# One fitted table of small steps for units 14 to 23, the change of stages and the first pass of the last stage of a linear-attention and MoE kernel

## The chip, the cores and the metric

The kernel runs on one core of a Trainium2 chip. The metric is device time in microseconds (us) of one execution, the median of three runs. The five engines of the core are named as the profile names them: PE (TensorE, matrix products; PEld is its loading of weights), DVE (VectorE), ACT (ScalarE), POOL (GpSimd) and SP (SyncE, which here issues most of the transfers). PSUM is the memory that PE writes into, eight banks of 128 x 512 floats; SBUF is the working memory of all the engines.

## The reference

Three layers, each fed by the one before; 3072 tokens (4 sequences of 768) of 384 values:

```python
# linear attention with a decaying state, 8 heads of 48
cur = einsum('bhd,bhe->bhde', u[None] * kt, vt)
y[:, :, t] = einsum('bhd,bhde->bhe', rt, state + cur)
state = wt[:, :, :, None] * state + einsum('bhd,bhe->bhde', kt, vt)
...
# layer 1: 384 -> 1024 -> 384
h = x @ w_in
e = exp(h - max(h));  sm = e / (sum(e) + 1e-09)
solu = h * sm
ln = (solu - mean(solu)) / sqrt(var(solu) + 1e-06) * g_ln
x = ln @ w_out
...
# layer 2: 384 -> 2048 -> 384
h = x @ w_in
g = maximum(0.01 * h, h)
out = g @ w_out
```

The weights of both layers come as 64-bit floats.

## The kernel before

**Number format.** Every large product is made in three passes: each operand is split into a high part (a rounded copy) and a low part (the rest), and high x high, low x high and high x low are added up in PSUM. A layer's weights come as pairs of 32-bit words and are decoded on the chip, slice by slice of 128 x 384 values: `decode_exp` (one operation on DVE, L114, then one on ACT, L116), `decode_sign` (DVE L120), `decode_top` (DVE L125), `decode_sum` (DVE L131), `decode_mul` (DVE L136), then a copy to the high part on ACT (L772) and a subtraction on DVE for the low part (L773). Layer 2 has 32 such slices, 16 of `w_in` and 16 of `w_out`. A raw slice sits in one of 4 buffers `w2s`, its decoded value in one of 3 buffers `w2t`.

**Units.** The tokens go through attention and layer 1 in 24 units of 128. A unit's steps are small functions. Preparation of decays and keys (`prep1` to `prep4`, `prep_state` and others) is made two or three units ahead, on DVE, ACT and POOL. Then come the attention products on PE (`att_scores`, `att_mid`, `att_y`, `att_state`), the sum `x` (`att_x`), its transpose and split (`x_t`, `x_hi`, `x_lo`), and layer 1's first product (`mm1`, 18 matmuls, L566) into the PSUM tile PH. On this stand the softmax and its statistics: `soft_max` (DVE), `soft_e` (ACT), `soft_z` (DVE), `soft_nm` (POOL), `soft_c` (ACT), `soft_q` (ACT). The result is transposed into the two banks PZ (`z_t`, eight transposes, L596) and split (`z_hi` on ACT L605, `z_lo` on DVE L609). For each group g of three units, layer 1's second product (`mm2`, L619) is made for three row blocks m of 24 matmuls each, some units later; `mm2_out` stores it to memory.

**Last stage.** Layer 2 has 96 items n, each a pair (g, c) of a group of 512 tokens and a block of 128 of the 2048 inner values. Items 0 to 31 alternate between groups 0 and 1 while the weights are decoded (the first pass); items 32 to 95 go through groups 2 to 5 one by one. An item is `mm3` (9 matmuls into a bank h, L794), 0.01 h on ACT (L801), the maximum on DVE (L802), the high part `gh` on ACT (L803), the low part `gw` on DVE (`gw_sub`, L808), and `mm4` (9 matmuls into three accumulator banks, L818), which stands two items later in PE's order.

**What sets the order.** The kernel is recorded with a manual schedule: each engine executes its instructions in the order in which the code calls the steps, and waits where an operand is not ready. Units 0 to 9 are ordered by a fitted table, the string `FIRST`. Units 10 to 22 repeat one line of steps, `LOOP`. Unit 23 and the change of stages (the last two softmaxes, `mm2` of the blocks 19 to 23, the closing and opening of memory pools, the first slices of layer 2's weights) are written out by hand, and the last stage is a loop whose body holds, for each of the 96 items,

```python
dec_step()
mm3(g, c)
gw_sub(g, c)
...
if 2 <= n < len(order) - 1:
    mm4(*order[n - 2])
```

where `dec_step` issues the whole decoding of one slice (its L114 and the second half of the slice before) as one block. Two PSUM pools of the last stage (two banks h, two sets of three accumulators) are opened when the pool of the units is closed.

Of the kernel before, what the change touches and what calls it, by code (L numbers as in the profile page):

```python
# [19 lines left out]
TOK = B * S  # L20
# [10 lines left out]
FIRST_UNITS = 10  # L31
FIRST = """
# [51 lines left out]
z_lo -1 0; z_lo -1 1; soft_q -1; prep_bonus 3; prep_check 3; mm1 0 0; mm1 0 1; prep1 3; prep2 3; prep_k 3  # L84
"""
# [225 lines left out]
def body(tc, trw, nat_q, nat_v, w1p, u_p, g_p, r, k, v, w, u, w1i, w1o, gln, w2i, w2o, out):  # L311
# [6 lines left out]
    with ExitStack() as ctx:  # L318
# [221 lines left out]
        def att_x(i):  # L540
            x = ap2.tile([128, H, D], F32, name="x")
# [171 lines left out]
        es2 = ExitStack()  # L713
        x2, acc, gs = {}, {}, {}
        lp_at = []
        wl = [("i", c) for c in range(3)]
        for c in range(K2):
            wl += [("o", c)] + [("i", c + 3)] * (c + 3 < K2)
        wd, wa, ws = [], [], []
        w2o_at, xhl2 = [], []  # L720

        def load_w2():
            if not wl:
                return
# [36 lines left out]
        def split_hi():
            if not ws or (ws[0][0] == "o" and ws[0][1] >= 4 * len(w2o_at)):
                return None
            s, c, t = ws.pop(0)
# [18 lines left out]
        def x2_lo(g, eng):  # L783
            xh, xl = x2[g]
            eng.tensor_tensor(out=xl, in0=f(xl), in1=f(xh), op=ALU.subtract)  # L785

        def mm3(g, c):
            xh, xl = x2[g]
            h2 = ps_h.tile([128, 512], F32, name="h2")
            v, o = divmod(c, 4)  # L790
            q = 0
            for kc in range(KC):
                for a, d in passes(w2i_h[v], w2i_l[v], xh, xl):
                    pe.matmul(out=h2, lhsT=a[:, kc, 128 * o:128 * o + 128], rhs=d[:, kc],  # L794
                              start=(q == 0), stop=(q == 8))
# [36 lines left out]

        with tc.manual_schedule():
# [25 lines left out]
            def mm2_of(i):  # L859
# [198 lines left out]
```

## Time and profile before

| | |
|---|---|
| median of three runs | 783.81 us (782.85 to 786.02) |
| the profiled execution | 783.52 us |
| its span, first to last instruction | 781.8 us |
| mean granted clock of PE | 0.988 |
| PE busy with matmuls | 730.4 us, 93% of the span |
| DVE busy | 518.5 us, 66% |
| ACT, POOL busy | 354.2 us and 162.6 us |

The profile is of one execution. The span is what the engines' records cover; 1.7 us of the execution's time lie around it. "Busy" is the time in which at least one instruction of the engine runs; matmuls overlap one another, so that a stretch in which PE shows no idle time can still take longer than its matmuls need. The granted clock is the share of TensorE's full clock that the chip allowed. In the middle of the kernel five points of the program are used as borders: 218.10 us, where the attention output of unit 14 begins, 326.70 us, where `mm1` of unit 22 begins, 366.04 us, where the last stage's first `mm3` begins, 494.20 us, where `mm3` of item 28 begins, and 776.00 us, the end of PE's work.

### The profile page before, as it was taken

Reading aid. Unit: us, or ns where it says so; the run is one execution under the profiler, and the core shown is the slowest. Engines: PE = TensorE matmul, PEld = TensorE weight load, DVE = VectorE, ACT = ScalarE, POOL = GpSimd, SP = SyncE. Lnnn points to the kernel's source line nnn. Section 1 sums busy time; section 2 is a strip of 40 time slices with the busy share of each in tenths; the row PEclk is TensorE's granted clock in tenths of the full one; section 3 lists DMA queues with packets and bytes.
Section 4 is the critical chain, followed back from the end, with each engine's and each line's share of the span. In section 5 each row is a group of like instructions: output and inputs, shape, how many; then the busy total and the mean of one; then the engine's idle time right before and its main releaser. Section 6 shows DMA issues by size and latency. Waiting matters only on the chain.

```text
span 781.8 us, 14968 instructions
## 1 busy us (share of the span) xinstructions
PE 730.4 (93%) x6197; PEld 612.9 (78%) x6197; DVE 518.5 (66%) x866; ACT 354.2 (45%) x648; POOL 162.6 (21%) x181
## 2 busy tenths in 40 slices
PE   2688999999999999989979999999999999999996
PEld 1366789898989999879758866788888888888885
DVE  6999889787888888577888888553343334334333
ACT  2557564666556465464444444433323322333231
POOL 2331554445555464002000000100100100100000
PEclk9999999999999999998989999999999999999999
DMA  9652335345354541035334221130002001001001
GB/s 299 201 164 71 99 102 161 92 139 146 98 161 127 164 117 48 22 92 162 91 113 162 81 81 41 37 125 1 0 3 79 0 1 42 0 1 41 0 1 44
DMA packets 30189, 66.60 MB, mean 85 GB/s; under 512 B 3228, under 2 KB 15668, under 8 KB 29988
## 3 DMA queue, kind: packets, MB, share of 16 engines
q1 hardware_dynamic: 29300, 62.45, 26.2%
q10 hardware_dynamic: 816, 3.15, 1.2%
q8 instruction: 50, 0.82, 0.5%
q14 instruction: 23, 0.19, 0.1%
HBM read 56.13 MB, written 9.45 MB: 84 GB/s over the span
## 4 chain that ended last, share of the span: by engine, by line
PE 72%; DVE 18%; issue 4%; ACT 3%; DMA 2%; POOL 0%; DVEq 0%; ACTq 0%; POOLq 0%
PE acc L818 18%; PE h L794 18%; PE PH L566 12%; PE PO L619 11%; PE PZ L596 3%; PE PZ L528 2%; DVE t L802 2%; ACT gh L803 2%; DVE w2s L131 2%; DVE w2t L120 2%; DMA ub<-in_u_p_dram 2%; PE PZ L537 1%; PE PA L465 1%; DVE gw L808 1%; DVE w2s L125 1%
## 5 line engine op out<-in xcount | busy, mean ns | idle before, releaser
L802 DVE TENSOR_TENSOR t<-t,h 128x512 f32<-128x512 f32 x96 | 65.8, 685 | 122.8 <-ACT t L801 122.8
L794 PE MATMUL h<-x2h,w2ih 128*128 128x512 f32 x288 | 114.8, 399 | 7.2 <-DVE t L802 7.0
L801 ACT ACTIVATE t<-h 128x512 f32<-128x512 f32 x96 | 57.1, 595 | 136.8 <-PE h L794 136.8
L808 DVE TENSOR_TENSOR gw<-t,gh 128x512 fp32r<-128x512 f32 x96 | 69.3, 722 | 65.9 <-ACT gh L803 65.9
L794 PE MATMUL h<-x2l,w2ih 128*128 128x512 f32 x288 | 112.7, 391 | 0.0
L794 PE MATMUL h<-x2h,w2il 128*128 128x512 f32 x288 | 112.7, 391 | 0.0
L818 PE MATMUL acc<-gw,w2oh 128*128 128x512 f32 x288 | 112.5, 391 | 0.0
L818 PE MATMUL acc<-gh,w2ol 128*128 128x512 f32 x288 | 112.5, 391 | 0.0
L818 PE MATMUL acc<-gh,w2oh 128*128 128x512 f32 x288 | 112.5, 390 | 0.0
L803 ACT CAST gh<-t 128x512 fp32r<-128x512 f32 x96 | 59.6, 621 | 93.8 <-DVE t L802 93.8
L785 POOL TENSOR_TENSOR x2l<-x2l,x2h 128x1536 fp32r<-128x1536 f32 x4 | 14.0, 3510 | 298.1 <-ACT x2h L781 298.1
L794 PEld LDWEIGHTS h<-x2h,w2ih 128*128 128x128 f32 x288 | 54.4, 189 | 25.8 <-DVE t L802 15.1
L794 PEld LDWEIGHTS h<-x2h,w2il 128*128 128x128 f32 x288 | 54.4, 189 | 11.5
L818 PEld LDWEIGHTS acc<-gh,w2ol 128*128 128x128 f32 x288 | 54.4, 189 | 11.3
L818 PEld LDWEIGHTS acc<-gw,w2oh 128*128 128x128 f32 x288 | 54.2, 188 | 11.3
L794 PEld LDWEIGHTS h<-x2l,w2ih 128*128 128x128 f32 x288 | 54.5, 189 | 10.8
L818 PEld LDWEIGHTS acc<-gh,w2oh 128*128 128x128 f32 x288 | 54.2, 188 | 11.2
L566 PE MATMUL PH<-w1ih,xh 128*128 128x512 f32 x144 | 59.2, 411 | 3.9 <-DVE zbuf L578 3.4
L619 PE MATMUL PO<-zh,w1oh 128*128 128x384 f32 x168 | 59.9, 357 | 0.0
L566 PE MATMUL PH<-w1ih,xl 128*128 128x512 f32 x144 | 57.2, 397 | 0.8 <-DVE xl L558 0.8
L566 PE MATMUL PH<-w1il,xh 128*128 128x512 f32 x144 | 57.1, 397 | 0.0
L619 PE MATMUL PO<-zh,w1ol 128*128 128x384 f32 x168 | 56.4, 336 | 0.0
(154 smaller groups left out, 1432.2 us busy)
## 6 DMA issues: line engine op xcount, KB each, us to landing
tr<-in_trw_dram SPq DMA_DIRECT2D x23, 675.9 KB, 5.5
natq<-in_nat_q_dram SPq DMA_DIRECT2D x24, 384.0 KB, 5.5
w2s<-in_moe_w_in_dram SPq DMA_DIRECT2D x48, 128.0 KB, 2.3
w2s<-in_moe_w_out_dram SPq DMA_DIRECT2D x16, 384.0 KB, 3.1
natv<-in_nat_v_dram SPq DMA_DIRECT2D x24, 192.0 KB, 3.8
o_dram<-o SPq DMA_DIRECT2D x24, 192.0 KB, 1.9
x2l<-o_dram SPq DMA_DIRECT2D x6, 768.0 KB, 5.3
out_dram<-ot SPq DMA_DIRECT2D x18, 256.0 KB, 2.1
```

The costliest lines, as they stand in the source:

```text
L120: nc.vector.scalar_tensor_tensor(out=t, in0=q[:, :, 1], scalar=-2147483648, in1=t, op0=ALU.bitwise_and, op1=ALU.bitwise_or)
L131: nc.vector.scalar_tensor_tensor(out=f(lw), in0=lw.bitcast(U32), scalar=2.0 ** -32, in1=q[:, :, 1], op0=ALU.mult, op1=ALU.add)
L528: pe.matmul(out=y[64 * c:64 * c + 64, hs], lhsT=s[64 * c:64 * c + 64, x, q], rhs=a[64 * c:64 * c + 64, h], start=(h == 0), stop=False, ski ...
L566: pe.matmul(out=PH[:, half], lhsT=a[:, kc], rhs=c[:, kc, 512 * half:512 * half + 512], start=(n == 0), stop=(n == 8))
L596: pe.transpose(PZ[c // 4][:, 128 * (c % 4):128 * (c % 4) + 128], zbuf[:, 128 * c:128 * c + 128], ident)
L619: pe.matmul(out=o2[m], lhsT=a[:, c, 128 * m:128 * m + 128], rhs=d[:, c], start=(c == 0 and q == 0), stop=(c == K1 - 1 and q == 2))
L794: pe.matmul(out=h2, lhsT=a[:, kc, 128 * o:128 * o + 128], rhs=d[:, kc], start=(q == 0), stop=(q == 8))
L801: act.activation(out=t, in_=h2, func=AF.Copy, scale=0.01)
L802: dve.tensor_tensor(out=t, in0=t, in1=h2, op=ALU.max)
L803: act.copy(out=gh, in_=t)
L808: dve.tensor_tensor(out=gw, in0=t, in1=f(gh), op=ALU.subtract)
L818: pe.matmul(out=at, lhsT=a[:, c % 4, 128 * o:128 * o + 128], rhs=d, start=(c == 0 and q == 0), stop=(c == K2 - 1 and q == 2))
```

## The change

A second table, `LAST`, takes the place of `LOOP` for units 14 to 22, of the hand-written code for unit 23 and the change of stages, and of the loop for items 0 to 33 of the last stage. Its steps are smaller: a slice's decoding is eight steps (`w2_load`, `w2_a` the exponent, `w2_e` the sign, `w2_f` the top, `w2_h` the sum, `w2_b` the product, `w2_c` the high part, `w2_d` the low part), an item's work between its two products is four (`g_min`, `g_max`, `g_hi`, `g_lo`), and `mm3`, `mm4`, the opening of pools, the loads of `x2` and the two small computations `flag` and `scale` are steps of their own, in any order that the table names. From item 34 on the loop is as it was.

Beside the order: PSUM is one pool, the last stage uses banks of the units' tiles (h: PK and one of PZ; accumulators: PH, the other PZ, PO and PA); `mm2` of the blocks 19, 21 and 23 uses PA in place of PK; `w2t` has 4 buffers (3), `x` one (2), `t` 2 and `gh`, `gw` 3 each throughout; one pair of the weight tiles stands in another pool; the last two `mm4` take their accumulators in the order 1, 2, 0.

```diff
+LAST_UNITS = 14
+N_LAST = 34
+N_RP = 4
...
+LAST = """
+soft_max 13; att_u 15; soft_e 13; w2_load 0; prep3 16; att_scores 15; att_y 14; load_nat 17; att_x 14; mm2a 14; x_t
...
+soft_e 23; z_lo 22 0; mm2b 24; z_hi 22 1; w2_f 6; soft_z 23; z_lo 22 1; soft_nm 23; soft_c 23; z_t 23; w2_e 7; w2_h
+5; mm2_out 24; z_hi 23 0; z_lo 23 0; w2_f 7; x2_hi 0; z_hi 23 1; flag_b; mm2a 25; flag_c; soft_q 23; w2_h 6; w2_b 5;
+z_lo 23 1; mm2b 25; w2_b 6; w2_load 8; open_xp; x2_lo 0; w2_h 7; mm3 0; mm2a 26; w2_b 7; w2_c 4; g_min 0; scale_a;
+w2_d 4; g_max 0; load_x2 1; x2_hi 1; mm2b 26; g_hi 0; w2_c 5; w2_c 6; w2_a 8; x2_lo 1; w2_load 9; w2_d 5; mm3 1; mm3
...
+g_max 11; w2_b 18; g_hi 10; w2_load 21; w2_c 17; mm4 9; g_lo 10; w2_d 17; w2_f 19; g_min 12; g_max 12; g_hi 11; w2_h
+19; w2_a 21; g_lo 11; mm3 13; w2_c 18; w2_load 22; w2_e 20; g_hi 12; w2_b 19; w2_f 20; w2_h 20; mm3 14; w2_e 21;
...
 def mm2(g, m, part):
     zh, zl = zg[g]
     if part == 0:
-        o2[m] = (PK if 3 * g + m in (19, 21, 23) else PO)[:, 0:384]
+        o2[m] = (PA[:, 0] if 3 * g + m in (19, 21, 23) else PO)[:, 0:384]
...
+        h_at = [PK, PZ[1]]
+        acc_at = [[PH[:, 0], PH[:, 1], PZ[0]], [PO, PA[:, 0], PA[:, 1]]]
...
+        def g_min(n):
+            p = pools["rp" if n < N_RP else "lp"]
+            gs[n] = [p.tile([128, 512], d, name=x, bufs=2 if x == "t" else 3)
+                     for x, d in (("t", F32), ("gh", F32R), ("gw", F32R))]
+            act.activation(out=gs[n][0], in_=h_at[n % 2], func=AF.Copy, scale=0.01)
+
+        def g_max(n):
+            t = gs[n][0]
+            dve.tensor_tensor(out=t, in0=t, in1=h_at[n % 2], op=ALU.max)
+
+        def g_hi(n):
+            t, gh, _ = gs[n]
             act.copy(out=gh, in_=t)
-            gs[g, c] = (gh, gw, t)
...
+        def g_lo(n):
+            t, gh, gw = gs[n]
             dve.tensor_tensor(out=gw, in0=t, in1=f(gh), op=ALU.subtract)
...
             run(FIRST)
-            for i in range(FIRST_UNITS, NU - 1):
-                if 15 <= i < 19:
-                    load_w2()
+            for i in range(FIRST_UNITS, LAST_UNITS):
                 run(LOOP, i)
...
-            for n in range(len(order)):
...
-                dec_step()
-                mm3(g, c)
-                gw_sub(g, c)
...
+            run(LAST)
+            for n in range(N_LAST, len(order)):
                 g, c = order[n]
-                if 2 <= n < len(order) - 1:
-                    mm4(*order[n - 2])
+                mm3(n)
+                g_min(n)
+                g_max(n)
+                g_hi(n)
+                g_lo(n)
```

Three places show what this does to DVE's order. The first is the first pass of the last stage. Before, DVE's order there repeats this block once for every item (L114 to L136 and L773 decode a slice, L802 is the maximum and L808 the low part `gw`):

```order
L114 TENSOR_SCALAR w2t<-w2s 128x384
L120 SCALAR_TENSOR_TENSOR w2t<-w2s,w2t 128x384
L125 TENSOR_SCALAR w2s<-w2s 128x384
L131 SCALAR_TENSOR_TENSOR w2s<-w2s 128x384
L136 SCALAR_TENSOR_TENSOR w2t<-w2s,w2t 128x384
L773 TENSOR_TENSOR w2il_4332<-w2t,w2ih_4331 128x3x128
L802 TENSOR_TENSOR t<-t,h_4998 128x512
L808 TENSOR_TENSOR gw<-t,gh 128x512
```

In the changed kernel the same operations (L195, L201, L206, L212 and L217 decode, L844 is a slice's low part, L907 the maximum, L915 the low part `gw`) stand in the same region like this, around the maxima of two successive items:

```order
L195 TENSOR_SCALAR w2t<-w2s 128x384
L907 TENSOR_TENSOR t<-t,PZ_100 128x512
L844 TENSOR_TENSOR w2il_4540<-w2t,w2ih_4539 128x3x128
L212 SCALAR_TENSOR_TENSOR w2s<-w2s 128x384
L915 TENSOR_TENSOR gw<-t,gh 128x512
L217 SCALAR_TENSOR_TENSOR w2t<-w2s,w2t 128x384 x2
L201 SCALAR_TENSOR_TENSOR w2t<-w2s,w2t 128x384
L907 TENSOR_TENSOR t<-t,PK 128x512
L206 TENSOR_SCALAR w2s<-w2s 128x384
L195 TENSOR_SCALAR w2t<-w2s 128x384
L212 SCALAR_TENSOR_TENSOR w2s<-w2s 128x384
L844 TENSOR_TENSOR w2ol_4756<-w2t,w2oh_4755 128x384
```

Between an item's maximum and its low part there now stand operations of other slices and other items, where nothing stood before, and the operations of several slices in work are mixed instead of one slice being decoded in one block.

The second is in the units, from the softmax maximum of unit 19 on (L571; L543 and L544 make `x` of unit 20, L578 is `soft_z`, L558 `x_lo`, L474 and L497 belong to the attention, L397 to L445 to the preparation of later units). Before:

```order
L571 TENSOR_REDUCE nmax<-PH 128x1
L543 TENSOR_TENSOR x<-PZ_99,vd 128x384
L544 TENSOR_TENSOR x<-PZ_100,x 128x384
L474 COPY_PREDICATED ss_122<-mask,PA 128x512
L578 SCALAR_TENSOR_TENSOR zbuf,z_all<-PH,ebuf 128x1024
L497 TENSOR_TENSOR ao<-PA,ae 112x192
L415 SCALAR_TENSOR_TENSOR e_3885<-tr,e_112 112x520
L558 TENSOR_TENSOR xl<-PZ_99,xh 128x384
L424 TENSOR_TENSOR lt<-tr,e_3885 112x512
L445 TENSOR_REDUCE dg<-natq 128x8
```

In the changed kernel, from the same softmax maximum on (L652, with L624 and L625 for `x`, L659 for `soft_z`, L639 for `x_lo`, L555 and L578 for the attention, L478 to L496 for the preparation), and with L201 and L206 of two slices' decoding:

```order
L652 TENSOR_REDUCE nmax<-PH 128x1
L201 SCALAR_TENSOR_TENSOR w2t<-w2s,w2t 128x384
L206 TENSOR_SCALAR w2s<-w2s 128x384
L624 TENSOR_TENSOR x<-PZ_99,vd 128x384
L625 TENSOR_TENSOR x<-PZ_100,x 128x384
L659 SCALAR_TENSOR_TENSOR zbuf,z_all<-PH,ebuf 128x1024
L484 RECIPROCAL e_112<-suf 112x8
L578 TENSOR_TENSOR ao<-PA,ae 112x192
L555 COPY_PREDICATED ss_122<-mask,PA 128x512
L496 SCALAR_TENSOR_TENSOR e_3923<-tr,e_112 112x520
L639 TENSOR_TENSOR xl<-PZ_99,xh 128x384
L478 SCALAR_TENSOR_TENSOR suf<-tr,sel 112x520
```

Steps of layer 2's decoding, which before stood in the change of stages and behind it, now stand among those of the units. The third place is PE's order at the change of stages, of which the lines of the table in the diff above tell all: before, `mm3` of item 0 stood behind the last `mm2`; now it stands ahead of `mm2` of the blocks 22 and 23 (`mm2a 26` to `mm2b 27`).

## Rows read from the trace of the kernel before

**Rows 1.** Head of the page and its part 1, busy time by engine.

```profile
span 781.8 us, 14968 instructions
...
PE 730.4 (93%) x6197; PEld 612.9 (78%) x6197; DVE 518.5 (66%) x866; ACT 354.2 (45%) x648; POOL 162.6 (21%) x181
```

**Rows 2.** Windows view: length, busy of PE, PEld, DVE, ACT, POOL, clock, DMA share, GB/s.

```profile
105.06:167.85 62.79, 61.30 (x924) 54.85 (x923) 52.39 (x81) 36.98 (x73) 28.29 (x37) 1.00 0.42 122
218.10:326.70 108.60, 108.60 (x1663) 99.56 (x1663) 86.24 (x131) 60.00 (x114) 51.78 (x56) 1.00 0.37 106
326.70:366.04 39.34, 36.18 (x245) 33.42 (x243) 27.64 (x53) 20.27 (x35) 0.47 (x2) 0.91 0.34 106
366.04:494.20 128.16, 118.45 (x489) 91.58 (x489) 106.83 (x217) 57.64 (x109) 4.20 (x1) 0.97 0.30 94
494.20:776.00 281.80, 281.56 (x1242) 232.85 (x1241) 109.61 (x158) 90.11 (x144) 14.04 (x4) 1.00 0.07 24
350.90:356.50 5.60, 5.60 (x20) 5.60 (x19) 5.02 (x10) 2.56 (x4) 0.00 (x0) 0.50 0.77 237
```

**Rows 3.** Timeline of PE in the change of stages: start, busy, operation, idle before.

```profile
337.33 1.09 PE L596 MATMUL PZ<-ident,zbuf 128*128 128x128 f32 x8 [0.24 <-ACT zbuf L586]
...
342.39 0.33 PE L619 MATMUL PO<-zh,w1oh 128*128 128x384 f32 x1
...
346.40 0.34 PE L619 MATMUL PO<-zh,w1ol 128*128 128x384 f32 x1
347.93 1.09 PE L596 MATMUL PZ<-ident,zbuf 128*128 128x128 f32 x8 [1.20 <-ACT zbuf L586]
350.75 0.19 PE L937 MATMUL PA<-ones,anyf 128*1 128x1 f32 x2 [1.73 <-DVE anyf L936]
```

**Rows 4.** Chain of the last stage's steady part: start, length, piece.

```profile
496.28 2.04 PE acc L818 x9
```

**Rows 5.** Timeline of DVE in the last stage's first pass.

```profile
384.80 0.69 DVE L808 TENSOR_TENSOR gw<-t,gh 128x512 fp32r<-128x512 f32 x1 [0.69 <-ACT gh L803]
385.41 0.35 DVE L114 TENSOR_SCALAR w2t<-w2s 128x384 int32<-128x384 int32 x1
...
387.73 0.55 DVE L773 TENSOR_TENSOR w2il<-w2t,w2ih 128x384 fp32r<-128x384 f32 x1
388.20 0.68 DVE L802 TENSOR_TENSOR t<-t,h 128x512 f32<-128x512 f32 x1
389.56 0.69 DVE L808 TENSOR_TENSOR gw<-t,gh 128x512 fp32r<-128x512 f32 x1 [0.69 <-ACT gh L803]
```

**Rows 6.** Waits view, first pass of the last stage: total, times, longest.

```profile
DVE gw L808 <- ACT gh L803: 17.9, 26, 0.7
...
PE h L794 <- DVE t L802: 7.0, 16, 1.3
```

**Rows 7.** Timeline of PE: where attention's output of two successive units begins.

```profile
306.01 0.27 PE L518 MATMUL PZ<-zero 48*64 48x192 bf16 x2
318.57 0.27 PE L518 MATMUL PZ<-zero 48*64 48x192 bf16 x2
```

**Rows 8.** Windows view of the table at the kernel's start, columns as above.

```profile
20.00:80.00 60.00, 45.42 (x612) 32.43 (x611) 58.37 (x107) 36.85 (x76) 17.08 (x21) 0.97 0.48 148
```

**Rows 9.** Groups by line, window 20 to 80 us: count, busy, mean ns.

```profile
L424 DVE TENSOR_TENSOR lt<-tr,e 112x512 f32<-112x512 f32 x4 | 2.7, 682 | 0.0
```

**Rows 10.** The same group, window 218.1 to 326.7 us.

```profile
L424 DVE TENSOR_TENSOR lt<-tr,e 112x512 f32<-112x512 f32 x8 | 7.7, 968 | 0.0
```

**Rows 11.** DMA issues of the page: count, KB each, us to landing.

```profile
w2s<-in_moe_w_out_dram SPq DMA_DIRECT2D x16, 384.0 KB, 3.1
...
x2l<-o_dram SPq DMA_DIRECT2D x6, 768.0 KB, 5.3
```

**Rows 12.** Groups by line, window 218.1 to 326.7 us.

```profile
L609 DVE TENSOR_TENSOR zl<-PZ,zh 128x512 fp32r<-128x512 f32 x16 | 10.3, 686 | 2.7 <-ACT zh L605 2.7
...
L605 ACT CAST zh<-PZ 128x512 fp32r<-128x512 f32 x17 | 9.2, 589 | 0.0
```

More of the change, by code (lines that the diff above doesn't have):

```diff
@@ new lines @@
+soft_max 20; soft_q 19; att_state 20; prep_vd 21; att_scores 22; att_u 22; prep_diag 22; att_y 21; att_x 21; soft_e
+20; soft_z 20; mm2_out 20; w2_b 2; w2_load 5; att_kt 23; w2_c 0; prep2 23; mm2a 21; x_t 21; mm2b 21; x_hi 21; w2_d
+0; x_lo 21; soft_nm 20; att_mid 22; att_evac_s 22; soft_c 20; w2_c 1; mm2_out 21; mm1 21 0; prep_vd 22; prep3 23;
+soft_q 20; z_t 20; prep_state 23; mm1 21 1; w2_f 3; att_mul_next 22; z_hi 20 0; z_lo 20 0; z_hi 20 1; att_evac_k 23;
+att_u 23; w2_a 4; z_lo 20 1; prep4 23; att_y 22; att_scores 23; prep_bonus 23; w2_e 4; prep_check 22; soft_max 21;
@@ new lines @@
+w2_d 1; att_x 22; soft_e 21; mm2a 22; x_t 22; w2_load 6; soft_z 21; w2_a 5; soft_nm 21; att_evac_s 23; x_hi 22; x_lo
+22; w2_f 4; w2_h 3; mm2b 22; mm1 22 0; mm2_out 22; prep_diag 23; w2_b 3; prep_vd 23; w2_load 7; w2_e 5; soft_c 21;
+att_mid 23; att_mul_next 23; z_t 21; z_hi 21 0; z_hi 21 1; z_lo 21 0; mm1 22 1; prep_check 23; z_lo 21 1; att_y 23;
+soft_q 21; flag_a; soft_max 22; att_x 23; mm2a 23; att_state 21; x_t 23; w2_c 2; w2_h 4; w2_b 4; soft_e 22; open_rp;
+x_hi 23; soft_z 22; w2_c 3; x_lo 23; mm2b 23; w2_d 2; load_x2 0; mm2_out 23; w2_a 6; w2_d 3; soft_nm 22; mm1 23 0;
@@ new lines @@
+2; w2_d 6; w2_load 10; w2_c 7; mm2_out 25; g_min 1; w2_e 8; w2_load 11; w2_f 8; w2_h 8; g_lo 0; w2_a 9; g_max 1;
+w2_e 9; w2_f 9; g_min 2; g_max 2; g_hi 1; w2_a 10; w2_b 8; mm3 3; mm2_out 26; g_lo 1; g_hi 2; w2_c 8; mm3 4; mm2a
+27; w2_d 7; mm4 0; w2_h 9; w2_a 11; w2_e 10; w2_d 8; g_lo 2; w2_f 10; w2_b 9; w2_h 10; w2_e 11; w2_b 10; g_min 3;
+w2_c 9; w2_c 10; mm2b 27; w2_load 12; w2_load 13; g_max 3; w2_a 12; mm2_out 27; w2_f 11; w2_d 9; w2_e 12; open_lp;
+w2_h 11; g_min 4; w2_a 13; g_max 4; w2_load 14; w2_b 11; w2_f 12; w2_c 11; g_hi 3; mm3 5; w2_e 13; w2_h 12; g_lo 3;
@@ new lines @@
+w2_load 28; w2_h 25; w2_d 23; g_lo 17; mm3 19; mm3 20; w2_f 26; mm4 16; g_min 19; w2_a 27; g_lo 18; w2_h 26; w2_b
+25; g_max 19; mm4 17; w2_c 24; mm3 21; g_hi 19; g_min 20; g_max 20; w2_load 29; mm3 22; g_lo 19; mm4 18; w2_c 25;
+w2_d 24; g_min 21; g_hi 20; mm4 19; w2_b 26; w2_e 27; w2_d 25; w2_a 28; w2_c 26; w2_load 30; g_lo 20; g_max 21;
+g_min 22; w2_a 29; g_max 22; mm3 23; g_hi 21; mm3 24; w2_e 28; g_lo 21; w2_f 27; w2_h 27; w2_d 26; mm4 20; w2_f 28;
+w2_b 27; g_min 23; g_max 23; mm4 21; g_hi 22; w2_e 29; g_lo 22; g_min 24; w2_c 27; w2_h 28; mm3 25; g_max 24; w2_d
@@ L85 @@
+g_hi 30; g_lo 30; g_min 31; g_min 32; g_max 31; g_max 32; g_hi 31; mm3 33; g_lo 31; w2_d 31; mm4 30; g_min 33; g_hi
+32; g_max 33; g_hi 33; g_lo 32; load_x2 3; g_lo 33; mm4 31
 """
@@ L761, in split_hi, with w2_a, w2_e, w2_f @@
[L761 to L764, printed above, removed]
+                sp.dma_start(out=raw[n], in_=words(w2o[128 * c:128 * c + 128]))
+        def w2_a(n):
+            val[n] = we.tile([128, DM], I32, name="w2t", bufs=4)
+            decode_exp(nc, raw[n], val[n], ebias)
+        def w2_e(n):
+            decode_sign(nc, raw[n], val[n])
+        def w2_f(n):
+            decode_top(nc, raw[n])
```

311 lines of the change are left out of this document (141 added, 170 removed).

## The prediction

> **What bounds the kernel now.** I read the head of the page first: over the whole span of 781.8 us PE shows matmuls for 730.4 us, DVE is busy for 518.5 us [rows 1]. PE is the bound on average, but the average hides stages, so the next view is the windows cut at the borders that the change moves [rows 2]. From 218.10 to 326.70 us PE is busy for all of the 108.60 us, DVE for 86.24: a unit there costs what PE needs, 12.56 us from one attention output to the next [rows 7]. From 494.20 us on PE is busy for 281.56 of 281.80 us, and the chain there is PE alone, nine matmuls in 2.04 us after nine matmuls [rows 4]. Between these two stretches lie 39.34 us of the change of stages and 128.16 us of the last stage's first pass, and only there is anything to be had.
>
> In the change of stages the timeline of PE shows the places [rows 3]. PE waits 0.24 us ahead of the transposes of unit 22. After a block of 24 matmuls, first at 342.39, last at 346.40 us (24 in 4.18 us, 0.174 us each), the next work could begin at 346.57 and begins at 347.93 us: 1.36 us lost on the softmax of unit 23. The eight transposes that follow take as long as those of unit 22 did until `mm1` took over (337.33 to 338.18, so 0.85 us); the small flag product then begins at 350.75 in place of 348.80 us: 1.95 us. Right behind this idle time the granted clock falls to the lower of its two levels, half speed (1.2 in place of 2.4 GHz): in the 5.60 us from 350.90 on there are 20 matmuls, which at 0.174 us would take 3.5 us [rows 2, 3]. That is 2.1 us; the mean clock of the whole stretch, 0.91 of 39.34 us, allows 3.5; I take 2.7. Sum of the losses: 0.24 + 1.36 + 1.95 + 2.7 = 6.3 us.
>
> In the first pass, 28 `mm3` and 26 `mm4` begin between 366.04 and 494.20 us: 54 items of 2.04 us [rows 4] are 110.2 us, and the stretch takes 128.16 [rows 2]: 18.0 us lost, 4.77 us for a pair in place of 4.08. DVE sets this pace: the timeline shows its low parts `gw` at 384.80 and 389.56 us, 4.76 apart, with no gap except 0.69 us ahead of each, in which it waits for ACT's high part `gh` of the same item [rows 5]; the waits view has 26 such waits, 17.9 us in all, nearly the whole of the 18.0 [rows 6]. PE in turn waits for DVE's maximum, which frees the bank h: 7.0 us in 16 waits [rows 6]. So a serial hand-off, maximum to `gh` to `gw`, is paid once per item by the engine that sets the pace.
>
> Matmul records overlap, and PE's busy time in this window is 118.45 us [rows 2]; read by that, only 128.16 - 118.45 = 9.7 us could be won. The Trainium skill (Perfetto Trace Analysis, section Identifying the Most-Contended Engine) says that matmul busy time is no good measure of how near PE is to its limit, and that the busy time of weight loads is. By this rule PE's work here is 91.58 us at the steady stretch's share of 232.85 in 281.80, or 110.8 us, and 17.3 us are to be had; the trace agrees, since the count above gives 18.0.
>
> **The change part by part.** *What it removes.* If DVE never waits and PE is always fed, the stretch from 326.70 to `mm3` of item 28 falls by 6.3 + 18.0 = 24.3 us. Against the profiled execution's own 783.5 us (span 781.8 and 1.7 around it), this is a floor of 759.2. The median of the runs is 0.3 us above the profiled execution, which is nothing.
>
> *What it adds.* No arithmetic: the same 32 slices, the same items. It is DVE's load that decides whether PE can be fed. From 218.10 to 494.20 us DVE is busy for 86.24 + 27.64 + 106.83 = 220.7 us [rows 2]; the floor of this stretch is 276.1 - 24.3 = 251.8, so DVE would be 88% busy. By parts: ahead of the first `mm3` the table decodes 8 slices, two more than before, some 2.4 us of DVE each from 385.41 to 388.20 us [rows 5] less the part of a slice that overlaps, so 86.24 + 27.64 + 4.8 = 118.7 us. PE's time there is 147.94 - 6.3 less the 8.35 us of two blocks of `mm2` that now stand behind the first `mm3`, 133.3 us: 89%. The rest is 102 of 118.5 us, 86%. A table has been seen to run DVE fuller than this: 58.37 of 60.00 us near the kernel's start [rows 8], there with DVE and not PE as the bound.
>
> *What it moves.* `mm4` of an item stands not two but up to five items behind its `mm3`, so 12 to 20 us of PE work lie between the two, in which 0.01 h, maximum, `gh` and `gw` fit (0.6 + 0.69 + 0.6 + 0.69 us [rows 5, 12], with the waits for their turn). Between maximum and `gw` stand 1 to 6 us of other DVE work, so the 0.69 us of [rows 6] lie under it: cost nothing. If this cover is gone somewhere, it is 0.69 us per place. The decoding's hand-offs to ACT (the exponent, the high part) are covered in the same way by operations of other slices. A raw slice's buffer comes free at `w2_b` of the slice four ahead; from there to `w2_a` lie 2.8 us of DVE work at the least and mostly 5 to 11, against 3.1 us for a transfer [rows 11]: at most 0.3 us once, not carried. SP's queue holds only such loads, the stores of `mm2_out` and the two loads of `x2`, and none of them waits for something late. `x` with one buffer must wait for the transpose of the unit before, long over; nothing. PA in place of PK for three blocks of `mm2`: the attention's last use of PA, `att_mid 23`, stands well ahead of `mm2a 23` in the table; nothing. The order of the last two `mm4`: at most the length of one output, 0.1 us.
>
> *What stays or comes.* (1) `z_t 23` is followed on PE by `mm2a 25`, which reads z of unit 23. Its first half goes through ACT (0.589) and DVE (0.686 us [rows 12]) while half of the transposes, 0.43 us, go on: 0.8 us of wait. (2) The softmax of unit 23 stands behind less PE work than in the units; between nothing and the 1.36 us of before: 0.4. (3) `x2` of group 1 is loaded behind `open_xp`: 5.3 us [rows 11], then a high and a low part of three times 512 values each, at most 3 x 0.589 and 3 x 0.686 us [rows 12], 9.1 in all, against 8.3 us of PE work (`mm2b 25`, `mm3 0`, `mm2` of block 22) up to `mm3 1`: 0.8, between 0 and 2. (4) Items 1 to 4 have four `mm3` in a row on two banks h; a bank comes back after 0.6 + 0.69 us, inside the 2.04 us of the other bank's `mm3`, if ACT and DVE are at hand; between 0 and 2 us, I take 0.8. (5) The rest of 300 steps in a fixed order: the units without a table lose nothing visible on PE, so 0 to 4; I take 1.5. Sum 4.3 us. Predicted: 783.5 - 24.3 + 4.3 = **763.5 us**.
>
> **The rivals.** *DVE slows down beside GpSimd.* The decoding's operations now stand in the units, where POOL is busy for 51.78 of 108.60 us; in the first pass it was for 4.20 of 128.16 [rows 2]. One DVE operation with two SBUF operands shows what this can mean: 682 ns in one window, 968 in another with more POOL work [rows 9, 10]. Ahead of the first `mm3` the table has 27 decoding operations with two SBUF operands (8 `w2_e`, 8 `w2_h`, 7 `w2_b`, 4 `w2_d`); at 0.29 us more each they take 7.7 us more, and DVE's 118.7 of 133.3 us become 126.4, 95%, near the fullest seen. With no slack left, half or all of it shows: 3 to 8 us over the forecast, 766.5 to 771.5. The Trainium skill (SBUF — State Buffer, section SBUF: two separate sides) says that DVE with two SBUF inputs and a GpSimd operation reading SBUF lock each other out for a whole instruction. By that rule these 27 operations are exposed; the difference between the two rows agrees with it.
>
> *Only the change of stages gains.* If the table's first pass keeps DVE's 4.77 us for a pair, because its hand-offs are late again, 783.5 - 6.3 = 777 to 778 us. For it: two banks h as before. Against it: other work stands between maximum and `gw`.
>
> *No change.* What the first pass and the change of stages give is lost in units 14 to 22, which had nothing to lose but DVE's slack: 780 to 787.7. A drop of the clock there, as the one at 350.90 us, costs 2.1 to 3.5 us each time; some six would be needed.
>
> *Slower.* The order of each engine is now rigid at 132 hand-offs from DVE to ACT and back (32 from `w2_a` to `w2_e`, 32 from `w2_c` to `w2_d`, 34 from `g_min` to `g_max`, 34 from `g_hi` to `g_lo`). If the real durations differ so that each shows the 0.69 us of [rows 6], that is 91 us of DVE standing still. DVE has 251.8 - 220.7 = 31 us to spare, or up to 63, since records overlap by 0.08 us (384.80 + 0.69 against 385.41 [rows 5]) in some 400 instructions; with 47, 44 us are lost against 24.3 won: 803 us. It decides from a mean wait of (47 + 24.3) / 132 = 0.54 us on. Against it: one such wait per item is all that the worst stretch of before shows.
>
> **How the numbers follow.** The forecast, 760 to 766.5 us, has 0.58; DVE beside GpSimd 0.23; only the change of stages 0.05; no change 0.06; slower 0.08. A measurement of this kernel can tell about 0.5%, 3.9 us, from no change, so faster is below 779.9 us: 0.58 + 0.23 + 0.05 = 0.86; same 0.06; slower 0.08. The range from 759.5 (the floor) to 773 us holds the first two cases with their bounds, 0.81.
>
> **What would show it.** Right: PE's busy share near 1.00 in every window from unit 14 to item 34; item 28's `mm3` some 20 us earlier; no `gw` wait of 0.69 us per item; DVE near 88% from unit 14 on; no second half-speed stretch of the clock. The sizes of (1) to (4) are the idle times ahead of `mm2a 25`, `mm3 1` and `mm3 3`. Wrong: DVE's decoding operations longer by 0.2 us or more in the units and PE waiting there for `soft_max`, `x_lo` or `z_lo`; or a period near 4.77 us for a pair in the first pass.

## The result and the profile after

The changed kernel takes 766.13 us (median of four runs, 764.97 to 767.82), the kernel before 784.74 us on the same chip (four runs, 782.85 to 786.02): ratio 0.9766, 95% interval 0.9736 to 0.9796, so 2.3% faster. Forecast were 763.5 us and a range of 759.5 to 773. The profiled execution has a span of 764.9 us in place of 781.8 [rows 1].

The windows of the changed kernel, with the columns of [rows 2] and its borders where they now lie (the output of unit 14, `mm1` of unit 22, the first `mm3`, `mm3` of item 28, the end of PE):

```profile
219.69:328.11 108.42, 107.53 (x1605) 97.63 (x1597) 93.62 (x154) 60.60 (x115) 42.53 (x53) 1.00 0.38 115
328.11:357.07 28.96, 26.91 (x204) 23.56 (x204) 20.85 (x39) 18.93 (x33) 1.97 (x4) 1.00 0.37 118
357.07:472.03 114.96, 114.96 (x518) 96.10 (x518) 98.09 (x203) 59.45 (x109) 7.97 (x2) 1.00 0.31 102
472.03:757.80 285.77, 285.76 (x1261) 236.30 (x1259) 111.47 (x164) 88.99 (x143) 10.54 (x3) 1.00 0.07 23
```

The reader is to see three things. The first pass (third line) is 13.2 us shorter than before, and PE has no idle time in it; since two blocks of `mm2` (8.35 us) moved into it and two `mm4` (4.08 us) out of it, the same work takes 114.96 - 8.35 + 4.08 = 110.7 us where it took 128.16: 17.5 of the 18.0 us are there. (PE's timeline of before has the first matmul of item 28's `mm3` at 493.94 us, so the border 494.20 lies 0.26 us inside it: by the item itself 17.2 of 17.7 us are there. Up to `mm3` of item 34, behind the same work in both kernels, it is 17.35 us.)

```profile
493.94 0.50 PE L794 MATMUL h<-x2h,w2ih 128*128 128x512 f32 x1
```

The clock is at full speed throughout. But the change of stages has idle time still, 28.96 against 26.91 us, and the units, which had none, now have 0.9 us.

DVE's timeline in the first pass shows what [rows 5] showed of before, two low parts `gw` (L915) that follow work without a wait, decoding ahead of each:

```profile
411.11 0.55 DVE L212 SCALAR_TENSOR_TENSOR w2s<-w2s 128x384 f32<-128x384 uint32 x1
411.58 0.35 DVE L195 TENSOR_SCALAR w2t<-w2s 128x384 int32<-128x384 int32 x1
411.85 0.68 DVE L915 TENSOR_TENSOR gw<-t,gh 128x512 fp32r<-128x512 f32 x1
...
415.66 0.55 DVE L844 TENSOR_TENSOR w2il<-w2t,w2ih 128x384 fp32r<-128x384 f32 x1
416.12 0.68 DVE L915 TENSOR_TENSOR gw<-t,gh 128x512 fp32r<-128x512 f32 x1
```

In the waits view from 357.07 to 455.71 us (items 0 to 24) the wait of [rows 6], once per item before, has shrunk to

```profile
DVE gw L915 <- ACT gh L911: 2.8, 4, 0.9
```

and PE waits for nothing in the first pass. Where the rest went, PE's timeline shows around `mm2` of block 21, the counterpart of [rows 3]:

```profile
349.01 1.09 PE L677 MATMUL PZ<-ident,zbuf 128*128 128x128 f32 x8 [0.28 <-ACT zbuf L667]
350.03 0.19 PE L936 MATMUL PA<-ones,anyf 128*1 128x1 f32 x2
350.34 0.45 PE L700 MATMUL PA<-zh,w1oh 128*128 128x384 f32 x1
351.06 0.45 PE L700 MATMUL PA<-zl,w1oh 128*128 128x384 f32 x1 [0.28 <-DVE zl L690]
...
353.59 0.41 PE L700 MATMUL PA<-zh,w1oh 128*128 128x384 f32 x1 [0.33 <-ACT w2oh L840]
355.03 0.44 PE L700 MATMUL PA<-zl,w1oh 128*128 128x384 f32 x1 [1.03 <-DVE zl L690]
...
357.07 0.39 PE L895 MATMUL PK<-x2h,w2ih 128*128 128x512 f32 x1
```

24 matmuls take 357.07 - 350.34 = 6.73 us in place of 4.17. DVE's timeline names what the last and longest of the three waits is for:

```profile
350.93 0.35 DVE L206 TENSOR_SCALAR w2s<-w2s 128x384 int32<-128x384 int32 x1
353.30 0.15 DVE L939 TENSOR_SCALAR flag<-PA 1x1 int32<-1x1 f32 x1 [2.02 <-PE PA L700]
353.37 0.54 DVE L212 SCALAR_TENSOR_TENSOR w2s<-w2s 128x384 f32<-128x384 uint32 x1
353.84 0.54 DVE L217 SCALAR_TENSOR_TENSOR w2t<-w2s,w2t 128x384 f32<-128x384 f32 x1
354.31 0.67 DVE L690 TENSOR_TENSOR zl<-PZ,zh 128x512 fp32r<-128x512 f32 x1
```

The flag is read from one element of PA, behind the first half of the `mm2` that writes to PA: DVE stands still for 2.02 us, and the low part of z that this same `mm2` needs for its second half stands behind the flag on DVE. The wait of 0.33 us ahead of the second half is put down to an ACT copy (L840) whose result that matmul does not read. In `mm2_first` below, with the same order there, the same wait is put down to the flag, since the second half writes to PA behind the flag's read:

```profile
355.11 0.41 PE L700 MATMUL PA<-zh,w1oh 128*128 128x384 f32 x1 [0.33 <-DVE flag L939]
```

### The profile page after: what moved, and what is told of

Its sections match the earlier page's. It is cut to its first block, busy times and chain, and to the rows that moved or that the text cites. A ratio compares the mean times of both kernels' runs of the same rounds, so it can differ in the third digit from the quotient of the medians.

```text
span 764.9 us, 14969 instructions
## 1 busy us (share of the span) xinstructions
PE 722.2 (94%) x6197; PEld 610.7 (80%) x6197; DVE 513.3 (67%) x866; ACT 354.0 (46%) x648; POOL 155.1 (20%) x181
## 3 DMA queue, kind: packets, MB, share of 16 engines
q10 hardware_dynamic: 816, 3.15, 1.2%
## 4 chain that ended last, share of the span: by engine, by line
PE 88%; DVE 7%; DMA 2%; issue 1%; ACT 1%; POOL 0%; ACTq 0%; DVEq 0%; POOLq 0%
PE PK L895 13%; PE PZ L895 13%; PE PH L647 12%; PE PO L700 11%; PE PA L924 9%; PE PH L924 9%; PE PO L924 4%; PE PZ L924 4%; PE PZ L677 2%; PE PZ L609 2%; PE PA L700 2%; DMA zh<-in_w1p_dram 2%; PE PA L546 2%; PE PZ L618 1%; PE PA L566 1%
## 5 line engine op out<-in xcount | busy, mean ns | idle before, releaser
L915 DVE TENSOR_TENSOR gw<-t,gh 128x512 fp32r<-128x512 f32 x96 | 68.4, 713 | 52.6 <-ACT gh L911 52.4
L907 DVE TENSOR_TENSOR t<-t,PZ 128x512 f32<-128x512 f32 x48 | 32.9, 686 | 68.8 <-ACT t L903 68.6
L907 DVE TENSOR_TENSOR t<-t,PK 128x512 f32<-128x512 f32 x48 | 33.0, 687 | 60.0 <-ACT t L903 59.8
L903 ACT ACTIVATE t<-PZ 128x512 f32<-128x512 f32 x48 | 28.7, 598 | 83.6 <-PE PZ L895 78.7
L903 ACT ACTIVATE t<-PK 128x512 f32<-128x512 f32 x48 | 28.7, 598 | 80.7 <-PE PK L895 76.4
L700 PE MATMUL PO<-zl,w1oh 128*128 128x384 f32 x168 | 56.3, 335 | 0.0
L895 PE MATMUL PK<-x2h,w2ih 128*128 128x512 f32 x144 | 56.2, 390 | 0.0
L895 PE MATMUL PZ<-x2h,w2il 128*128 128x512 f32 x144 | 56.1, 389 | 0.0
L895 PE MATMUL PZ<-x2l,w2ih 128*128 128x512 f32 x144 | 56.1, 389 | 0.0
L895 PE MATMUL PK<-x2h,w2il 128*128 128x512 f32 x144 | 56.0, 389 | 0.0
L895 PE MATMUL PK<-x2l,w2ih 128*128 128x512 f32 x144 | 56.0, 389 | 0.0
L895 PE MATMUL PZ<-x2h,w2ih 128*128 128x512 f32 x144 | 56.0, 389 | 0.0
L652 DVE TENSOR_REDUCE nmax<-PH 128x1 f32<-128x1024 f32 x24 | 29.3, 1219 | 13.7 <-PE PH L647 13.6
L690 DVE TENSOR_TENSOR zl<-PZ,zh 128x512 fp32r<-128x512 f32 x48 | 31.8, 682 | 8.5 <-ACT zh L686 8.4
```

What stands on the lines that cost most here:

```text
L652: dve.tensor_reduce(out=nmax[:, i:i + 1], in_=flat(PH), axis=AX.X, op=ALU.max, negate=True)
L690: dve.tensor_tensor(out=zl, in0=p, in1=f(zh), op=ALU.subtract)
L700: pe.matmul(out=o2[m], lhsT=a[:, c, 128 * m:128 * m + 128], rhs=d[:, c], start=(c == 0 and q == 0), stop=(c == K1 - 1 and q == 2))
L895: pe.matmul(out=h_at[n % 2], lhsT=a[:, kc, 128 * o:128 * o + 128], rhs=d[:, kc], start=(q == 0), stop=(q == 8))
L903: act.activation(out=gs[n][0], in_=h_at[n % 2], func=AF.Copy, scale=0.01)
L907: dve.tensor_tensor(out=t, in0=t, in1=h_at[n % 2], op=ALU.max)
```

## The experiments

The times below are medians beside the kernel before on the same chip. The start of the program (units 0 to 9) differs by up to 5.6 us between profiled executions of kernels with the same order there (attention output of unit 13 at 203.67 to 209.26 us), so places inside a trace are compared from unit 13 on: "late at item 34" is the time of its `mm3` against the changed kernel's, less the difference at unit 13.

**Does the order of the steps give the first pass's gain?** `first_serial` keeps banks, buffers and everything up to the first `mm3`, and gives each item behind it the order of before, so for item 8:

```diff
+w2_a 13; w2_c 11; w2_e 12; w2_f 12; w2_h 12; w2_b 12; w2_load 16; w2_d 11;
+mm3 8; g_min 8; g_max 8; g_hi 8; g_lo 8; mm4 6;
```

> Behind the first mm3 every item has the order of the kernel before again: one slice decoded as one block, then maximum, high part and low part with nothing between them, mm4 two items behind mm3; PSUM banks, buffers and everything ahead stay as in the changed kernel. If the order of the steps gives the gain of the first pass (theory): 24 items with a block fall back to the 4.77 us a pair of the kernel before, 24 x 0.69 = 16.6 us are lost, 781 to 784 us, and a wait of about 0.69 us for gh ahead of each gw is back. If the PSUM banks and buffers give it (rival): within 2 us of the changed kernel's 766.1.

Measured: 778.04 us, ratio 0.9936 (0.9912 to 0.9959); 11.5 us late at item 34. Its DVE timeline is that of [rows 5] again, period 4.77 us:

```profile
429.68 0.69 DVE L915 TENSOR_TENSOR gw<-t,gh 128x512 fp32r<-128x512 f32 x1 [0.69 <-ACT gh L911]
...
433.08 0.68 DVE L907 TENSOR_TENSOR t<-t,PZ 128x512 f32<-128x512 f32 x1
434.45 0.69 DVE L915 TENSOR_TENSOR gw<-t,gh 128x512 fp32r<-128x512 f32 x1 [0.69 <-ACT gh L911]
```

The order does it, not the banks or buffers. Less is lost than the 16.6 us of the theory, since here only the items 12 to 28 run at this pace (some 9.5 us for two, 8.16 before that).

**Is it the hand-off?** `serial_cover` is `first_serial` with one step moved per item:

```diff
-g_max 8; g_hi 8; g_lo 8; mm4 6; w2_a 14; w2_c 12; w2_e 13; w2_f 13; w2_h 13;
+g_max 8; g_hi 8; mm4 6; w2_a 14; w2_c 12; w2_e 13; g_lo 8; w2_f 13; w2_h 13;
```

> first_serial with one step moved: in the items 3 to 26 the low part stands behind the first two decoding operations of the next slice (0.35 + 0.55 us, which take no result of this item), no longer right behind the maximum; slices are still decoded one by one in a block, mm4 still stands two items behind. Theory (the uncovered 0.69 us hand-off is what makes a pair take 4.77 us): a pair takes the 4.08 to 4.2 us that PE needs, 8 to 11.5 us of the 11.5 us by which first_serial lies behind the changed kernel come back, 766.5 to 770 us. Rival (the hand-off is not the cause, or DVE without any slack keeps PE waiting all the same): 4.5 us or more a pair, 774 us and above.

Measured: 767.70 us, ratio 0.9781 (0.9748 to 0.9813); at item 34 it is 0.1 us late. Its DVE timeline:

```profile
429.73 0.35 DVE L195 TENSOR_SCALAR w2t<-w2s 128x384 int32<-128x384 int32 x1
430.00 0.55 DVE L201 SCALAR_TENSOR_TENSOR w2t<-w2s,w2t 128x384 int32<-128x384 int32 x1
430.51 0.69 DVE L915 TENSOR_TENSOR gw<-t,gh 128x512 fp32r<-128x512 f32 x1
...
434.59 0.69 DVE L915 TENSOR_TENSOR gw<-t,gh 128x512 fp32r<-128x512 f32 x1
```

The period is 434.59 - 430.51 = 4.08 us, what PE needs for an item's 18 matmuls [rows 4]. So the uncovered 0.69 us was the whole of `first_serial`'s loss, and two decoding operations between maximum and low part give all that the table gives there (with the table's banks and its first eight slices decoded ahead; the same move in the kernel before was not run).

**The same hand-off in the table's order.** `lo_behind_max` moves only `g_hi` and `g_lo`:

```diff
-g_min 12; g_max 12; g_hi 11; w2_h 19; w2_a 21; g_lo 11;
+g_min 12; g_max 12; g_hi 12; g_lo 12; w2_h 19; w2_a 21;
```

> Only the high and the low part of each of the items 0 to 33 move: they stand right behind the maximum, so that nothing covers the hand-off from DVE to ACT and back. DVE then stands still 34 x 0.69 = 23 us in a first pass in which it has some 17 us of idle time and waits for gh 5 us already. Theory (only what exceeds DVE's spare time shows): 0 to 6 us slower, 766 to 772. Rival (each such wait delays the bank h and mm3, as before, whatever DVE has to spare): 14 us or more slower, 780 and above.

Measured: 787.04 us, ratio 1.0039 (1.0020 to 1.0057); 18.9 us late at item 34. The rival. The waits view, from the first `mm3` to that of item 24, on DVE and on ACT, offered a second cause, the buffer of `gh`, which comes free with `mm4` three items back:

```profile
DVE gw L915 <- ACT gh L911: 23.7, 23, 6.0
...
ACT gh L911 <- PE PZ L924: 7.9, 2, 7.0
```

`lo_behind_max5` gives `gh` and `gw` five buffers (`bufs=2 if x == "t" else 3 if n < N_RP else 5`, and `ot` one).

> As lo_behind_max, with five buffers in place of three for the high and the low part from item 4 on (and one in place of three for the output tile, which costs a few us at the very end and nothing before it). If lo_behind_max was slow because the high part stood waiting for a free buffer while DVE waited behind it (theory): most of its 21.9 us at mm3 of item 34 come back, 0 to 6 us over the changed kernel's 500.6 us there. If the 0.69 us hand-off itself, uncovered 34 times, is the cost (rival): still 14 us or more late at item 34.

Measured: 795.17 us in one run; 13.1 us late at item 34 (behind that DVE waits 30.0 us in 13 places for the stores from the single `ot` buffer). Buffers were worth 5.8 of 18.9 us, the hand-off most of the rest. My theory failed on where DVE has room: up to item 24 it is busy for 87.2 of 98.6 us in the changed kernel, so 11.4 us are free there, not the 17 us of the whole stretch, of which its other waits need some, and the wait alone takes

```profile
DVE gw L915 <- ACT gh L911: 16.6, 23, 1.1
```

in the waits view of this kernel up to the same item.

**Is the distance on PE needed?** `mm4_two` puts `mm4 n` behind `mm3 n + 2` on PE and leaves the other engines' orders, but for `mm2_out 27`, `open_lp` and `scale_b`, which come earlier, as does `mm2` of block 23 on PE. PE's steps around item 26:

```diff
-mm3 25; mm3 26; mm4 22; mm4 23; mm3 27; mm3 28; mm4 24;
+mm4 22; mm3 25; mm4 23; mm3 26; mm4 24; mm3 27; mm4 25; mm3 28;
```

> PE's order alone goes back to mm4 of item n right behind mm3 of item n + 2; DVE's and ACT's orders stay, in which gw stands 1 to 6 us of other work behind the maximum. Theory (the distance on PE is what the loose order on DVE needs): PE waits for gw at many items, 4 to 15 us slower, 770 to 781. Rival (DVE's order alone does it, two items are far enough): within 2 us of 766.1.

Measured: 793.83 us, ratio 1.0144 (1.0099 to 1.0189); 26.9 us late at item 34. The theory's direction, nearly twice its size: PE waits 10.3 us for `gw` and `gh` (and 4.8 us for slices of `w_out` whose decoding is not done), and DVE then waits for maxima whose `mm3` stands behind the late `mm4` (between 357 and 500 us 30.7 us in 17 waits of `t` L907 for ACT's L903, whose own input is PE's `mm3`). `tight_both` joins the two edits:

> lo_behind_max and mm4_two together: each item again as in the kernel before (maximum, high part, low part with nothing between, mm4 two items behind), while the decoding keeps the mixed order of the table. Theory (what counts is that the orders of PE, DVE and ACT fit one another, and an item's uncovered hand-off on DVE): the result lies near first_serial, mm3 of item 34 at 508 to 516 us, total 774 to 782 us, so well below either of the two alone. Rival (each of the two costs what it cost alone): the losses add up, above 800 us.

Measured: 800.69 us in one run, 34.8 us late at item 34. The theory failed; the rival's time came by a hair, but its sum did not, since the two losses would be 18.9 + 26.9 = 45.8 us. With items as tight as those of `first_serial` this kernel loses 23 us more. Two items in `first_serial` take 8.16 to 9.58 us, here 8.16 to 14.65, and PE waits 10.4 us for maxima and 9.9 us for slices of `w_out`. My reading is that the uneven order of the decoding pays only with the distance on PE to even it out. That is argued from the periods and waits; no kernel here varies the evenness alone. The clock has a share too: from the first `mm3` to item 34 it stands at half speed for 17.1 us in `mm4_two` and 20.5 us in `tight_both`, in `first_serial` never, and such a stretch can cost up to half its length.

**What is the place of the decoding worth?** `late_decode` moves 33 steps of decoding (five slices) out of the units and spreads them evenly from `att_y 23` to `mm2a 24`; one of the places that they leave:

```diff
-soft_q 20; z_t 20; prep_state 23; mm1 21 1; w2_f 3; att_mul_next 22; z_hi 20 0;
+soft_q 20; z_t 20; prep_state 23; mm1 21 1; att_mul_next 22; z_hi 20 0;
```

> The 33 steps of decoding that the table puts among the units (five slices) move behind the attention output of unit 23, evenly spread up to mm2a 24; only the loads of the first four slices stay. Theory (DVE has room in the units, not in the change of stages): the units get back most of the 1.8 us by which they are slower than before, but some 11 us of DVE work more meet 7 us of spare time in the change of stages, and the first mm3 comes 3 to 8 us later: 768 to 774 us. Rival (decoding beside GpSimd in the units costs more than it hides): below 765 us.

Measured: 777.42 us, ratio 0.9910 (0.9878 to 0.9941). The units are 1.6 us faster, the first `mm3` is 9.3 us late (PE waits 3.2 us for `soft_z`, 2.6 and 2.4 us for `soft_c` and `x`, and the clock falls to half speed twice, 3.41 us each). Theory, with the loss a little above its bound: DVE's room in the units is worth 9 us, and costs 1.6.

**Can the rest be had?** `z23_first` mends the place that the profile after shows:

```diff
-z_hi 23 0; z_lo 23 0; w2_f 7; x2_hi 0; z_hi 23 1; flag_b; mm2a 25; flag_c; soft_q 23; w2_h 6; w2_b 5; z_lo 23 1;
+z_hi 23 0; z_lo 23 0; z_hi 23 1; z_lo 23 1; w2_f 7; x2_hi 0; w2_h 5; flag_b; mm2a 25; soft_q 23; w2_h 6; w2_b 5;
```

with `flag_c` behind `x2_lo 0`.

> The four splits of z of unit 23 stand together, ahead of the high part of x2 on ACT and of a slice's sum on DVE, and the flag on DVE, which reads PA behind the first half of mm2 of block 21, moves behind x2_lo 0. In the changed kernel this mm2 takes 6.7 us in place of 4.2 (waits for z_lo 23 0, z_hi 23 1 and z_lo 23 1). Theory: 1.7 to 2.3 us come back, the first mm3 at about 355 us, 764 us in all. Rival (x2_lo 0 is then late instead, as its high part starts 0.6 us later): less than 0.7 us.

Measured: 766.24 us, ratio 0.9780 (0.9756 to 0.9804). The first `mm3` is 1.9 us earlier, as expected, but item 34 only 0.7 (and the times show no gain): between items 16 and 24 PE waits for a `gw` that stands behind one slow operation. In the changed kernel the same operation is slow with nobody waiting; on DVE and POOL:

```profile
431.44 3.15 DVE L195 TENSOR_SCALAR w2t<-w2s 128x384 int32<-128x384 int32 x1 [0.43 <-DMA w2s<-in_moe_w_out_dram]
```

```profile
430.78 3.59 POOL L881 TENSOR_TENSOR x2l<-x2l,x2h 128x1536 fp32r<-128x1536 f32 x1 [67.45 <-ACT x2h L877]
```

A decoding operation of 0.35 us ends 0.2 us behind GpSimd's. `z23_x2late` moves GpSimd's behind the decoding, `after_again` is the changed kernel beside it:

```diff
-mm4 14; att_state 23; w2_load 26; w2_f 24; x2_hi 2;
+mm4 14; att_state 23; w2_load 26; w2_f 24;
...
-mm3 28; g_hi 26; w2_d 28; w2_h 30; x2_lo 2;
+mm3 28; g_hi 26; w2_d 28; w2_h 30; x2_hi 2; x2_lo 2;
```

> z23_first with the high part of x2 of group 2 moved from item 17 to item 28, so that GpSimd's low part of it, which starts as soon as the high part is there, no longer falls among the decoding. In the changed kernel a decoding operation of 0.35 us on DVE takes 3.15 us beside it; in z23_first PE then waits 0.8 us for a low part, and 1.07 us of its 2.5 us are given back there. Theory: the 1.07 us return, and mm3 of item 34, measured from unit 13, is 1.7 us earlier than in the changed kernel: 764 to 765 us. Rival (GpSimd then holds up another operation of DVE at the same cost): no gain over z23_first.

> The changed kernel itself, to have it beside z23_x2late on the same chip: 766.1 us, 0.977 of the kernel before; the theory of z23_x2late needs 1 us or more between the two, its rival none.

Measured: 764.63 us (0.9757, 0.9730 to 0.9784) and 765.50 us (0.9775, 0.9747 to 0.9803). From unit 13 to item 34 the trace shows 1.4 us less than in the changed kernel, and the 1.07 us are back; the times differ by 0.9 us, which the intervals cannot tell from nothing.

`best` is `z23_first` with each accumulator scaled right behind its own matmuls:

```diff
             for o in os:
...
-            if c == K2 - 1:
-                for o in os:
-                    ot = pools["lp"].tile([128, 512], F32, name="ot", bufs=3)
+                if c == K2 - 1:
+                    ot = pools["lp"].tile([128, 512], F32, name="ot", bufs=3)
```

> z23_first, and in the last mm4 of a group each accumulator is scaled and stored right behind its own matmuls, not behind those of all accumulators named. In the changed kernel PE's last matmul is 17.97 us earlier than before but the span ends only 16.91 us earlier: the first scaling starts 1.34 us ahead of PE's end in place of 2.0, and the last store is issued 0.76 us behind the one before. Theory: 0.5 to 1.1 us come back at the end, 762.5 to 763.5 us in all, the last store landing some 3.5 us after its issue. Rival (the end is the same): equal to z23_first.

Measured: 783.80 us, ratio 1.0005 (0.9989 to 1.0021). Both cases were wrong. In the profiled execution (span 776.2 us, shorter than the median's) PE now waits 12.4 us in six places for the scaling, as here:

```profile
500.81 0.72 PE L924 MATMUL PA<-gh,w2oh 128*128 128x512 f32 x1 [2.62 <-DVE ot L928]
```

Two accumulators are banks of one tile, PA or PH, and the next matmuls into the tile wait for DVE's reading of its other bank. So the shared banks have a price. The kernel before, with a tile for each accumulator, scaled each right behind its own matmuls; the changed kernel first makes all matmuls, and so does not pay this price. The timed runs lose some 5 us more than the profiled execution, and their mean granted clock is lower (777.87 us at 0.996, 781.29 at 0.990, 786.69 at 0.983); why it is lower in them stays open.

`mm2_first` puts all of layer 1's second product ahead of the first `mm3`:

```diff
+mm2a 26; mm2b 26; mm2_out 25; mm2a 27; mm2b 27; mm2_out 26; mm2_out 27;
 mm3 0;
-mm2a 26; ... mm2b 26; ... mm2_out 25; ... mm2a 27; ... mm2b 27; ... mm2_out 27;
```

> All of layer 1's second product stands ahead of the first mm3, as it had to before, when the last stage had PSUM pools of its own; everything else as in the changed kernel. Theory (the shared banks are worth the early start that they give DVE and ACT): DVE's 87 us of work up to item 24 meet 8.35 us less time, 90 us in place of 98.6, so that its slack is nearly gone: 2 to 6 us slower, 768 to 772 us. Rival (PE has the same work either way and nothing is late): within 1 us of 766.1.

Measured: 783.06 us, ratio 0.9970 (0.9948 to 0.9991); 15.1 us late at item 34, neither case. The chain of this kernel shows another cause:

```profile
367.67 0.32 SPq L706
367.99 0.05 issue
368.04 5.91 DMA x2l<-o_dram
```

My move put the three stores of `mm2_out` ahead of the load of `x2` on SP's queue: it is issued at 368.04 us, where the changed kernel issues it at 350.19. PE waits 6.3 us for it, and from 372.6 us on the clock stands at half speed for 10.24 us. What the shared banks themselves are worth stays open.

## Why the prediction was right

- **The 18.0 us of the first pass**: right, by the item's own start 17.7. 17.2 to 17.5 us came, the cause is the uncovered hand-off, shown by `first_serial` and `serial_cover`. The clock was another candidate, since [rows 2] has 0.97 there: from 404.3 to 411.1 us it was at half speed. But DVE's `gw` stay 4.77 us apart through it, except for one distance of 5.18 us (408.63 to 413.82), so that it cost 0.4 us. The estimate by the weight loads' busy time was 17.3 us, by the matmuls' 9.7. What came agrees with the rule of the Trainium skill (Perfetto Trace Analysis, section Identifying the Most-Contended Engine).
- **The 6.3 us of the change of stages less what stays**: the mechanism was right, the size was off. Terms (1), (2) and (5) of "what stays or comes" were put at 0.8 + 0.4 + 1.5 = 2.7 us. They measured 2.6 us (`mm2` of block 21: 6.73 against 4.17), 0.6 us (0.45 ahead of the transposes of unit 23 and 0.2 behind them), and 1.8 us in the units (127.0 from the output of unit 13 to that of unit 23, before 125.2), 5.0 in all. What (1) missed is the flag: its step was in the table with PA written ahead of it, and I had put the use of PA at nothing, having looked only for who else writes PA. `z23_first`, which takes the flag away from there and puts the splits together, gives 1.9 us back.
- **Terms (3) and (4)**: put at 1.6 us, measured at nothing. The load of `x2` is issued at 350.19 us, 13.2 us ahead of `mm3 1` (363.35 us), where the prediction counted 8.3 us of PE work against 9.1; `mm3` of the items 1 to 4 follow each other at 2.04 to 2.08 us.
- **The order of the last two `mm4`**: put at 0.1 us; no loss is to be seen. PE's last matmul, the last scaling and the issue of the last store are all 18.0 us earlier:

```profile
775.80 0.69 DVE L822 TENSOR_TENSOR ot<-acc,cb 128x512 f32<-128x512 f32 x1 [0.67 <-PE acc L818]
776.52 0.33 SPq L823 DMA_DIRECT2D out_dram<-ot  x1
```

```profile
757.83 0.69 DVE L929 TENSOR_TENSOR ot<-PO,cb 128x512 f32<-128x512 f32 x1
758.55 0.33 SPq L930 DMA_DIRECT2D out_dram<-ot  x1
```

  The span's end is only 16.9 us earlier because 6.35 us lie behind that issue, before 5.29. In the other ten runs with the same end of the program it is 5.35 to 6.30 us, so the end scatters by about as much with nothing changed in it. The theory of `best`, which put it down to the scaling, rested on a wrong reading.
- The sum: forecast 24.3 - 4.3 = 20.0 us. From unit 13 to item 34 it is 18.65, and the medians differ by 18.6; the two spans differ by 16.9, with 1.06 us less at the end and 0.7 at the start, where nothing was changed (`after_again` starts 1.1 us faster). That the total came so near is in part luck: (3) and (4), which cost nothing, made up for most of the 2.3 us that (1), (2) and (5) had too little.
- **DVE beside GpSimd**, given 0.23: the mechanism is there, its price a third of mine, concentrated in single operations. From the output of unit 13 to that of unit 23 L217, L201 and L212 have means of 920, 664 and 590 ns (4, 6 and 4 of them; I had taken all 27 up to the first `mm3` as slowed), in the first pass 551, 553 and 554: 2.3 us, in place of 7.7. The worst stands at 268.43 us beside GpSimd's, a low part of z behind it, and 0.81 us reach PE:

```profile
268.43 2.04 DVE L217 SCALAR_TENSOR_TENSOR w2t<-w2s,w2t 128x384 f32<-128x384 f32 x1
268.75 0.52 POOL L517 TENSOR_TENSOR ae<-st,suf 112x192 f32<-112x192 f32 x1
269.23 1.93 POOL L532 TENSOR_TENSOR vd<-natv,dg 128x384 f32<-128x384 f32 x2
...
271.20 0.24 PE L599 MATMUL PZ<-zero 48*64 48x192 bf16 x1 [0.81 <-DVE zl L690]
```

- **The slower rival** held that uncovered hand-offs decide. The table covers them, so it did not come; but with those of 34 items uncovered in the table's own order (`lo_behind_max`) the kernel is slower than before.

## What to carry to other kernels

Look for the wait that the engine setting the pace pays once per item, and put two operations of other work between its two ends: here one moved step per item gave in the first pass what the table's 420 steps there gave. An order is fitted as a whole: moving one engine's steps, or a store ahead of a load on a transfer queue, cost 15 to 27 us, well over what the sums of busy times had said, since free time counts only up to the item at which it is needed. When PSUM tiles are shared or joined, ask for each read of a tile which writes to its other parts stand ahead of it in the program.

## What the runs showed of the hardware that was not expected

- A DVE operation with a single SBUF operand (L195, 0.35 us) took 3.15 us beside a GpSimd operation of 3.59 us with two. The Trainium skill (SBUF — State Buffer, section SBUF: two separate sides) names DVE operations with two SBUF inputs or in a two-port performance mode as those that are locked out. With its one operand this one is not of the first kind; in which mode it ran no run here shows. That GpSimd's operation was the cause `z23_x2late` shows: with it moved away, none of the 32 operations of L195 that decode there takes longer than 1.06 us.
- The kernel's first 90 us are not the same twice: the granted clock stood at half speed there for 3.41 us in `after_again` and for 13.65 us in `serial_cover`, whose unit 13 comes 4.1 us later, with the same steps up to unit 23. That is more than `z23_x2late` gains.
